# Two expert-weight loads under way instead of three, logits copied as separate work, and a new order, in a linear recurrence with a routed mixture of experts

## The chip, the cores and the metric

The kernel runs on one core of a Trainium2 chip. The metric is the device time of one execution in microseconds (us), as the median of several executions. The core has five engines with a queue of instructions each: PE (TensorE, matmuls), DVE (VectorE), ACT (ScalarE), POOL (GpSimd) and SP (SyncE, which here only issues transfers). Sixteen DMA engines move the data. An engine runs its queue strictly in order and waits at an instruction whose inputs aren't there, so that the order of each queue is the schedule.

## The reference

Two stages follow each other. The first is a gated linear recurrence over 4 sequences of 5056 tokens with 256 channels; the second sends each of the 20224 tokens to the one of eight experts with the largest logit.

```python
# recurrence, per sequence, token by token (D = 256)
log_a = 8.0 * sigmoid(r_gate) * log(sigmoid(a_param))
a = exp(log_a)
h = a * h + sqrt(max(1 - a * a, 1e-6)) * sigmoid(i_gate) * x      # x_t of the second stage
# experts, E = 8, F = 1024
logits = X @ w_gate
e = argmax(logits)
p = softmax(logits)[e];  g = sigmoid(X @ w_output_gate)[e]
out = p * g * (relu(X @ w1[e]) @ w2[e])
```

## The kernel before

The tokens are handled in 20 chunks of 8 tiles of 128 tokens, two blocks of 512 tokens in each chunk. For a chunk, SP loads `rt`, `it` and `xt` of both blocks (half a megabyte each, L536). ACT makes the gates and the decay (tanh, exp), the square of the decay (L556) and, after a table load, the root (L561); DVE makes the gate product (L548), the inputs of the recurrence (L564) and the recurrence itself as a scan (L595). PE then transposes each tile of 128 tokens and computes its logits in the same matmuls (`project`, tile `prow`, L629; three places in PSUM). From `prow` DVE takes the largest absolute value (L643) and a scale (L645), ACT or DVE writes the upper half of the row (L654 or L652), and DVE the lower half (L658) into one of eight places in `rows_all`. Just ahead of the lower half the same piece of work copies the 16 logits to `lz` (L657). From the logits of a chunk DVE and PE find experts and ranks (`pk`, L696) and DVE the positions (`posi`, L734). POOL scatters the rows by these positions into `xs` in HBM, one indirect transfer per tile (L365). From chunk 2 on each scatter waits for the newest relu, which spreads them over the time ("paced").

The second stage runs in slots of up to 256 tokens of one expert, 114 in all. Slots 0 to 7 hold 128 tokens of each expert from chunk 0, slots 8 to 15 the same of chunk 1. Later slots are dynamic: a plan made by DVE says which expert and which rows, and three plans can be in being at a time. Chunk 3 begins with slot 21, chunk 6 with 39, and chunks 7 to 11 with 43, 47, 51, 55 and 59. For a slot, SP issues a transposing fetch of the rows (L872) and one of their scales (`mt`, L873), and for dynamic slots a copy of the expert's first weights (`ws`, two of half a megabyte, L898). PE computes H in eight parts (`ph`, 48 matmuls, L929), ACT and DVE split the relu of each part into two halves (L944, L947), PE computes the output (`po`, L982), ACT scales it (L994) and POOL stores the rows (L997).

The expert weights come as 16 units, w1 and w2 of an expert by turns, 1 MB each (L424). A unit is loaded, a matmul gram gives its scale, ACT or DVE writes its upper half (L487, L489, by `MODES`: S is ACT, D is DVE), and DVE its lower half (L497). Load u waits on SP for the landing of load u - `DEPTH`, and what is behind it on SP waits too. The first 14 loads stand ahead of slot 0's fetch; the last two are staged in other places.

The order of every queue comes from a planner (`in_order`), which simulates engines and places pieces of work by rank, with durations and a table of ranks in the constants at the file's head: ranks of units, chunks, slots and loads, the slack that a projection is given, the engine of early squares and upper halves by chunk (`SQUARES`, `UPPERS`; A is ACT, D is DVE), and the chunks whose roots don't wait for both blocks (`ALONE`).

## Time and profile before

| | |
|---|---|
| median of three runs | 1082.36 us (1080.93 to 1087.27) |
| profiled execution | 1081.11 us, of which the span of the trace is 1079.4 us |
| granted PE clock, mean | 0.969 of full speed |
| PE busy | 1001.5 us, 93% |
| DVE busy | 772.4 us, 72% |
| ACT busy | 642.5 us, 60% |
| POOL busy | 361.7 us, 34% |
| moved by DMA | 250.94 MB |

The shares are means over the span. PE is far from full in the first 200 us, has a gap near 300 us, and is nearly full from there to the last 20 us. A share therefore says little here, and the rows further down go by stage. In a row of a timeline, the bracket at its end gives how long the engine had been idle, and what ended that.

### The profile page before, as it was taken

To read this page: it belongs to the slowest core of one execution; us is meant where nothing else is said; L and a number is where in the kernel's file an instruction comes from. 1 tells how busy PE (TensorE), PEld (TensorE's weight loads), DVE (VectorE), ACT (ScalarE), POOL (GpSimd) and SP (SyncE) were. 2 spreads that over 40 slices of the span, in tenths; PEclk is the share of its full clock that TensorE was granted. 3 is DMA by queue.
4 is the path that set the end of the run, shared out by engine and by line. 5 is a ranking of instruction groups with operands and counts; after the bars stand their busy time and mean duration, and the time that the engine had idled before them with its cause. 6 is when DMAs were issued, how large, how long until landed. Compare 5 with 4: busy or idle time off the path is not lost.

```text
span 1079.4 us, 31430 instructions
## 1 busy us (share of the span) xinstructions
PE 1001.5 (93%) x10506; PEld 910.0 (84%) x10506; DVE 772.4 (72%) x2324; ACT 642.5 (60%) x1153; POOL 361.7 (34%) x348
## 2 busy tenths in 40 slices
PE   3459799999989999999999999999999999999997
PEld 2358699888979889898998889889889888899996
DVE  6898989877768878888878878868776433233443
ACT  7668686867475575775776676765763323233332
POOL 1313324524324333343343343344353442121111
PEclk9659799999989999999999999999999999999999
DMA  9996447989979978879789889868855655378784
GB/s 330 382 334 131 140 121 193 239 280 291 307 211 296 258 240 261 262 228 263 238 242 265 247 239 253 252 219 259 219 178 173 190 186 157 137 223 245 240 244 125
DMA packets 200763, 250.94 MB, mean 232 GB/s; under 512 B 122108, under 2 KB 133118, under 8 KB 200608
## 3 DMA queue, kind: packets, MB, share of 16 engines
q1 hardware_dynamic: 184720, 205.55, 65.9%
q0 software_dynamic: 15888, 43.31, 12.5%
q8 instruction: 99, 1.62, 0.6%
q14 instruction: 56, 0.46, 0.1%
HBM read 79.09 MB, written 46.23 MB: 116 GB/s over the span
## 4 chain that ended last, share of the span: by engine, by line
PE 59%; issue 10%; DMA 10%; DVE 9%; POOL 5%; ACT 4%; SPq 1%; POOLq 0%; ACTq 0%; DVEq 0%
PE ph L929 27%; PE po L982 27%; PE prow L629 5%; DMA xs<-rows_all,posi 3%; POOL xs L365 3%; DVE it L595 2%; POOL out_dram L997 2%; DVE h L947 2%; DMA rt<-in_r_gate_dram 2%; DMA w2r<-in_moe_w_dram 1%; DMA ws<-w1r 1%; DMA w1r<-in_moe_w_dram 1%; DMA xt<-xs 1%; DVE it L564 1%; ACT h L944 1%
## 5 line engine op out<-in xcount | busy, mean ns | idle before, releaser
L982 PE MATMUL po<-w2r,h 128*128 (+1 forms) x3936 | 533.3, 274 | 3.5 <-ACT ot L994 1.3
L929 PE MATMUL ph<-xt,ws 128*128 128x256 f16 (+1 forms) x4704 | 484.3, 247 | 5.1 <-DMA ws<-w1r 2.1
L929 PEld LDWEIGHTS <-ws 128*128 128x128 f16 x4704 | 384.4, 98 | 42.1 <-issue 4.6
L982 PEld LDWEIGHTS <-h 128*128 128x128 f16 x3936 | 374.4, 98 | 45.4 <-issue 4.9
L947 DVE SCALAR_TENSOR_TENSOR h<-ph,h 128x256 f16<-128x256 f32 (+1 forms) x456 | 240.1, 537 | 217.6 <-ACT h L944 187.8
L944 ACT ACTIVATE h<-ph 128x256 f16<-128x256 f32 (+1 forms) x456 | 211.8, 474 | 243.1 <-PE ph L929 150.4
L997 POOL DMA_INDIRECT out_dram<-ot,mt x164 | 180.9, 1103 | 434.6 <-ACT ot L994 313.9
L365 POOL DMA_INDIRECT xs<-rows_all,posi x158 | 168.5, 1066 | 264.3 <-ACT h L944 173.2
L629 PE MATMUL prow<-iw,it 128*128 128x144 f32 x632 | 113.5, 305 | 19.7 <-DVE rows_all L658 9.9
L629 PEld LDWEIGHTS prow<-iw,it 128*128 128x128 f32 x632 | 92.4, 202 | 25.9 <-issue 10.3
L654 ACT ACTIVATE rows_all<-prow,sc 128x256 f16<-128x256 f32 x150 | 67.3, 474 | 64.0 <-DMA xs<-rows_all,posi 27.9
L994 ACT ACTIVATE ot<-po,osc 128x256 f32<-128x256 f32 x164 | 71.9, 471 | 54.9 <-PE po L982 49.4
L595 DVE TENSOR_TENSOR_SCAN it<-rt,last,it 128x512 f32<-128x512 f32 (+4 forms) x78 | 96.3, 1242 | 0.3
L658 DVE SCALAR_TENSOR_TENSOR rows_all<-prow,sc,rows_all 128x256 f16<-128x256 f32 x158 | 75.2, 477 | 0.0
L643 DVE TENSOR_REDUCE am<-prow 128x1 f32<-128x256 f32 x158 | 61.4, 418 | 17.4 <-PE prow L629 12.5
L542 ACT ACTIVATE rt<-rt 128x1024 f32<-128x1024 f32 (+1 forms) x40 | 41.8, 1045 | 34.1 <-DMA rt<-in_r_gate_dram 31.6
L552 ACT ACTIVATE rt<-rt,lam 128x512 f32<-128x512 f32 (+1 forms) x80 | 61.7, 802 | 0.5
L929 PE MATMUL ph<-xt,w1r 128*128 128x128 f16 x768 | 55.3, 225 | 4.6 <-DVE h L947 2.6
L564 DVE SCALAR_TENSOR_TENSOR it<-it,xt 128x1024 f32<-128x1024 f32 (+1 forms) x40 | 48.3, 1207 | 15.5 <-ACT it L561 15.0
L929 PEld LDWEIGHTS <-w1r 128*128 128x128 f16 x768 | 50.6, 102 | 7.3 <-issue 6.0
L548 DVE SCALAR_TENSOR_TENSOR xt<-it,xt 128x1024 f32<-128x1024 f32 (+1 forms) x40 | 48.3, 1208 | 5.8 <-ACT it L545 4.9
L545 ACT ACTIVATE it<-it 128x1024 f32<-128x1024 f32 (+1 forms) x40 | 41.9, 1048 | 8.9 <-DMA it<-in_i_gate_dram 8.5
(132 smaller groups left out, 586.0 us busy)
## 6 DMA issues: line engine op xcount, KB each, us to landing
ws<-w1r SPq DMA_DIRECT2D x196, 512.0 KB
rt<-in_r_gate_dram SPq DMA_DIRECT2D x39, 512.0 KB
it<-in_i_gate_dram SPq DMA_DIRECT2D x39, 512.0 KB
xt<-in_x_dram SPq DMA_DIRECT2D x39, 512.0 KB
w1r<-in_moe_w_dram SPq DMA_DIRECT2D x7, 1024.0 KB
w2r<-in_moe_w_dram SPq DMA_DIRECT2D x7, 1024.0 KB
out_dram<-ot,mt POOLq DMA_INDIRECT x164
xs<-rows_all,posi POOLq DMA_INDIRECT x158
```

Source lines behind the costliest of these rows:

```text
L365: op = nc.gpsimd.indirect_dma_start(out=xs[:, :], out_offset=bass.IndirectOffsetOnAxis(ap=pos, axis=0), in_=rows.bitcast(F32), in_offset=None,
L552: nc.scalar.activation(r[:, h], r[:, h], AF.Exp, scale=lam[:, h:h + 1], bias=lam[:, h:h + 1])
L595: nc.vector.tensor_tensor_scan(H[:, h, lo:hi], A[:, h, lo:hi], H[:, h, lo:hi], first, op0=ALU.mult, op1=ALU.add)
L629: nc.tensor.matmul(pf[:, h * P:(h + 1) * P + 2 * E], lhsT=H[:, h, (j % 4) * P:(j % 4 + 1) * P], rhs=iw[:, h, :], start=h == 0, stop=h == N ...
L654: nc.scalar.activation(r4(j)[:, 0], pr(j), AF.Copy, scale=sc)
L658: nc.vector.scalar_tensor_tensor(r4(j)[:, 1], pr(j), st("sc", 1, I32)[:, j, :].bitcast(F32), r4(j)[:, 0], op0=ALU.mult, op1=ALU.subtract)
L929: nc.tensor.matmul(ph[:, i, 0:w], lhsT=ws[:, f // 2 % 2, a, c, i * P:(i + 1) * P], rhs=xt[:, b * ND + c, 0:w], start=k == 0, stop=k == 3 * ...
L944: newest["relu"] = nc.scalar.activation(part(0, f0), tiles["ph", s, f0][:, :, 0:w], AF.Relu).ins
L947: nc.vector.scalar_tensor_tensor(part(1, f0), tiles["ph", s, f0][:, :, 0:w], 0.0, part(0, f0), op0=ALU.max, op1=ALU.subtract)
L982: nc.tensor.matmul(po[0:pw, j], lhsT=hh[:, a, f % 4, j * P:j * P + pw], rhs=second(b), start=f + j + a + b == 0, stop=f == NF - 1 and a == ...
L994: nc.scalar.activation(ot[0:pw], tiles["po", s][0:pw, j], AF.Copy, scale=tiles["osc", s][0:pw, j, :])
L997: op = nc.gpsimd.indirect_dma_start(out=out[:, :], out_offset=bass.IndirectOffsetOnAxis(ap=tiles["mt", s][0:pw, j, 1:2].bitcast(I32), axis=0),
```

## The change

Five things change.

- `DEPTH` is 2 instead of 3: a load of expert weights waits for the landing of the load two before it.
- Six plans can be in being (`Ring(6)`, and six buffers of `plv` and `pvi`) instead of three.
- The copy of the logits is a piece of work of its own, placed by the planner, and on ACT for chunks 0, 1, 2 and 4.
- Squares of chunks 0 and 3 and the upper halves of chunk 1 go to DVE, and units 5 and 8 change the engine of their upper halves.
- Ranks, slacks and the planner's other numbers are new, and with them the order of all queues.

ACT has 4 squares fewer, 32 copies of 128x16 more, and 8 upper halves of rows fewer; DVE has 32 copies fewer, 4 squares and 8 upper halves of rows more, two upper halves of w1 units more and one of a w2 unit less. PE and SP have as many instructions as before.

```diff
-MODES = 'SDSSSDSSSSSDSSDS'
+MODES = 'SDSSSSSSDSSDSSDS'
-SQUARES = 'AAAAA'
-UPPERS = 'AAADA'
+SQUARES = 'DAADA'
+UPPERS = 'ADADA'
+LOGITS = 'AAADA'
-LAG = 0.00125
-ALONE = (2, 5)
+LAG = 0.00118
+ALONE = (2, 6, 7)
...
-UNIT_LOAD = (7.506, 26.722, 61.465, 7.528, 72.147, 27.72, 26.183, 77.196, 87.463, 88.003, 27.858, 54.286, 26.607, 77.269, 49.185, 26.095)
+UNIT_LOAD = (-9.843, 16.647, 12.279, -35.055, -33.379, -9.228, 66.192, 67.677, -10.911, -50.334, -19.806, -7.546, -56.85, 18.29, -40.9, 67.054)
...
-DEPTH = 3
-SLACK = (1.027, 1.107)
+DEPTH = 2
+SLACK = (0.348, 1.194)
...
-        "mt": Ring(6), "ot": Ring(2), "osc": Ring(4), "plan": Ring(3), "ps_h": Ring(3), "ps_o": Ring(2), "ps_r": Ring(3),
+        "mt": Ring(6), "ot": Ring(2), "osc": Ring(4), "plan": Ring(6), "ps_h": Ring(3), "ps_o": Ring(2), "ps_r": Ring(3),
...
+        copier = "ACT" if c < len(LOGITS) and LOGITS[c] == "A" else "DVE"
...
+                def logits(j=j):
+                    lz, at = st("lz", 2 * E)[:, j, :], tiles["prow", c, j][:, P:P + 2 * E]
+                    if copier == "ACT":
+                        nc.scalar.activation(lz, at, AF.Copy)
+                    else:
+                        nc.vector.tensor_copy(lz, at)
+
                 def lo(j=j, pr=pr, r4=r4):
-                    nc.vector.tensor_copy(st("lz", 2 * E)[:, j, :], tiles["prow", c, j][:, P:P + 2 * E])
...
+                        lows.append(work(copier, 0.22 if copier == "ACT" else 0.1, logits, [w] + chain["small"], rank + TAIL, uses=[pu]))
                         w = work("DVE" if c < len(UPPERS) and UPPERS[c] == "D" else "ACT", 0.37, hi, [t, old], rank + TAIL, uses=[pu, used])
-                        lows.append(work("DVE", 0.48, lo, [w], rank + TAIL, uses=[pu, used]))
+                        lows.append(work("DVE", 0.41, lo, [w], rank + TAIL, uses=[pu, used]))
```

What the new numbers do shows in the queues. Three places follow, in each the order before and then that of the change. In the change, lines of the kernel are numbered 2 to 10 higher.

On DVE at the start, before the change, this stands between the last lower half of chunk 0's rows (`prow_7`) and chunk 0's positions (`posi_431`).

```order
L658 SCALAR_TENSOR_TENSOR rows_all<-prow_7_322,sc_285,rows_all 128x256
L678 TENSOR_REDUCE mx_385<-lz_302 128x8
L679 TENSOR_TENSOR df_387<-lz_302,mx_385 128x64
L497 SCALAR_TENSOR_TENSOR w2r<-w2r,wsc 128x2048
L686 SCALAR_TENSOR_TENSOR eq_398<-df_387,rev 128x64
...
L707 TENSOR_REDUCE zs_404<-df_387 128x8
L497 SCALAR_TENSOR_TENSOR w1r<-w1r,wsc 128x4x256
L714 TENSOR_SCALAR zs_404<-zs_404 128x8
...
L734 TENSOR_REDUCE posi_431<-pos_428 128x8
```

With the change, from the bits of the first weight scales on.

```order
L491 TENSOR_SCALAR w2r<-w2r,wsc 128x2048
L499 SCALAR_TENSOR_TENSOR w2r<-w2r,wsc 128x2048
L499 SCALAR_TENSOR_TENSOR w1r<-w1r,wsc 128x4x256
...
L499 SCALAR_TENSOR_TENSOR w1r<-w1r,wsc 128x4x256
...
L550 SCALAR_TENSOR_TENSOR xt_0_248<-it_0_180,xt_0_248 128x1024
L550 SCALAR_TENSOR_TENSOR xt_4_270<-it_4_287,xt_4_270 128x1024
...
L499 SCALAR_TENSOR_TENSOR w1r<-w1r,wsc 128x4x256 x2
...
L499 SCALAR_TENSOR_TENSOR w2r<-w2r,wsc 128x2048
...
L744 TENSOR_REDUCE posi_493<-pos_490 128x8
```

Two gate products of chunk 1, three more lower halves of w1 and one more of w2 now stand ahead of chunk 0's positions. The upper half of w2 (L489, L491) stood ahead of them before too. On SP, the 14 weight loads ahead of slot 0's fetch have ten loads of chunks 1 and 2 among them with the change, where eight stood before; on PE, seven projections of chunk 1 stand ahead of slot 0's first matmul, where four stood before.

On PE near slot 30 (`xt_30`, `ws` of the slot), before the change, the fifth projection of chunk 6 (`prow_4`) stands between the last output matmul of slot 28 and the first H of slot 30.

```order
L982 LDWEIGHTS h_1_4676
L982 ISA
L982 MATMUL po_4687<-w2r,h_1_4676 128x256
L629 MATMUL prow_4_4861<-iw,it_4_3945 128x144 x2
L929 LDWEIGHTS ws_0_4700
L929 MATMUL ph_0_4867<-xt_30_4530,ws_0_4700 128x128
```

With the change it stands inside slot 31.

```order
L939 LDWEIGHTS ws_1_4927
L939 MATMUL ph_4_5043<-xt_31_4718,ws_1_4927 128x128
L632 MATMUL prow_4_5050<-iw,it_4_3934 128x144 x2
L992 LDWEIGHTS h_0_4901
L992 ISA
L992 MATMUL po_5004<-w2r,h_0_4901 128x256
```

It has moved by more than a slot, and the projections behind it with it.

On POOL, before the change, these are the eight scatters of chunk 11 (`posi_9222`) among the stores of slots 53 to 57 (`ot_0`, `ot_1` are the halves of a slot; a slot of 128 tokens has one).

```order
L997 DMA out_dram<-ot_1_9109,mt_8365 20224x256
L365 DMA xs<-rows_all,posi_9222 172032x264 x2
L997 DMA out_dram<-ot_0_9281,mt_8560 20224x256
L365 DMA xs<-rows_all,posi_9222 172032x264 x4
L997 DMA out_dram<-ot_0_9480,mt_8918 20224x256
L997 DMA out_dram<-ot_1_9483,mt_8918 20224x256
L365 DMA xs<-rows_all,posi_9222 172032x264 x2
L997 DMA out_dram<-ot_0_9691,mt_8970 20224x256
```

With the change they are `posi_9240`.

```order
L1007 DMA out_dram<-ot_1_9118,mt_8371 20224x256
L367 DMA xs<-rows_all,posi_9240 172032x264
L1007 DMA out_dram<-ot_0_9252,mt_8532 20224x256
L367 DMA xs<-rows_all,posi_9240 172032x264 x3
L1007 DMA out_dram<-ot_0_9429,mt_8971 20224x256
L1007 DMA out_dram<-ot_1_9441,mt_8971 20224x256
L367 DMA xs<-rows_all,posi_9240 172032x264 x4
L1007 DMA out_dram<-ot_0_9624,mt_9018 20224x256
```

One scatter stood before the store of slot 54 that now stands behind it, and four instead of two stand behind the stores of slot 55.

## Rows read from the trace of the kernel before

**Rows 1.** Busy time by stage: window, length, then us (x count) per engine, clock, DMA, GB/s.
```profile
0.00:75.00 75.00, 29.81 (x216) 26.41 (x217) 61.07 (x144) 52.41 (x75) 17.52 (x26) 0.74 1.04 347
75.00:140.00 65.00, 56.01 (x654) 51.49 (x653) 58.24 (x151) 49.56 (x92) 19.96 (x13) 0.88 0.56 149
140.00:200.00 60.00, 58.51 (x756) 54.54 (x755) 53.08 (x164) 44.59 (x82) 21.00 (x19) 1.00 0.67 167
290.00:320.00 30.00, 24.95 (x271) 22.44 (x269) 18.39 (x62) 16.62 (x33) 9.04 (x9) 0.89 0.79 218
400.00:640.00 240.00, 237.84 (x2295) 214.47 (x2293) 198.24 (x617) 159.94 (x273) 87.01 (x86) 1.00 0.88 250
```
**Rows 2.** The same view, of shorter stretches (PE, PEld, DVE, ACT, POOL, clock, DMA, GB/s).
```profile
25.00:45.00 20.00, 6.44 (x67) 5.46 (x68) 17.43 (x61) 9.88 (x21) 1.57 (x1) 0.78 1.07 375
45.00:75.00 30.00, 15.59 (x98) 13.80 (x96) 29.24 (x40) 23.12 (x32) 11.31 (x7) 0.50 1.10 343
300.00:310.00 10.00, 10.00 (x93) 9.15 (x94) 8.02 (x30) 5.38 (x10) 3.35 (x4) 0.71 0.35 134
```
**Rows 3.** Chain of work that ended last, around slot 0: start us, us, what.
```profile
53.16 9.57 DMA w1r<-in_moe_w_dram
...
63.42 9.54 DMA xt<-xs
...
73.00 1.44 PE ph L929 x12
```
**Rows 4.** Timelines of ACT and DVE, chunk 0's second square, root and inputs.
```profile
13.90 1.06 ACT L556 ACTIVATE it<-rt 128x1024 f32<-128x1024 f32 x1
...
16.27 2.19 ACT L561 ACTIVATE it<-it,quarter 128x1024 f32<-128x1024 f32 x2
...
17.45 1.23 DVE L564 SCALAR_TENSOR_TENSOR it<-it,xt 128x1024 f32<-128x1024 f32 x1 [3.73 <-ACT it L561]
```
**Rows 5.** Groups of DVE, 0 to 75 us: form, count, busy us, mean ns, idle before.
```profile
L497 DVE SCALAR_TENSOR_TENSOR w1r<-w1r,wsc 128x1024 f16<-128x1024 f32 x8 | 10.1, 1277 | 0.4 <-ACT w1r L487 0.4
L497 DVE SCALAR_TENSOR_TENSOR w2r<-w2r,wsc 128x2048 f16<-128x2048 f32 x4 | 9.4, 2348 | 0.0
...
L548 DVE SCALAR_TENSOR_TENSOR xt<-it,xt 128x1024 f32<-128x1024 f32 x5 | 6.1, 1221 | 3.4 <-ACT it L545 3.0 <-DMA xt<-in_x_dram 0.4
...
L657 DVE COPY lz<-prow 128x16 f32<-128x16 f32 x10 | 1.7, 168 | 0.0
```
**Rows 6.** Timeline of DVE: chunk 0's positions, and slot 0's first lower half of H.
```profile
41.06 0.17 DVE L714 TENSOR_SCALAR zs<-zs 128x8 f32<-128x8 f32 x1 [1.85 <-ACT zs L710]
...
42.33 0.22 DVE L734 TENSOR_REDUCE posi<-pos 128x8 int32<-128x64 f32 x1
...
74.96 0.42 DVE L947 SCALAR_TENSOR_TENSOR h<-ph,h 128x256 f16<-128x256 f32 x1
```
**Rows 7.** Timeline of POOL: first and last of chunk 0's eight scatters.
```profile
43.35 1.57 POOL L365 DMA_INDIRECT xs<-rows_all,posi  x1 [32.87 <-DVE tab L743]
...
57.41 0.96 POOL L365 DMA_INDIRECT xs<-rows_all,posi  x1 [0.30 <-issue]
```
**Rows 8.** Timelines of ACT and PE at the gap near 300 us.
```profile
298.22 0.47 ACT L654 ACTIVATE rows_all<-prow,sc 128x256 f16<-128x256 f32 x1 [3.27 <-DMA xs<-rows_all,posi]
...
299.95 1.33 PE L629 MATMUL prow<-iw,it 128*128 128x144 f32 x4 [3.09 <-DVE rows_all L658]
```
**Rows 9.** Timelines of ACT, POOL, SP and PE: chunk 11 from its last relu to slot 59.
```profile
561.44 0.60 ACT L944 ACTIVATE h<-ph 128x512 f16<-128x512 f32 x1
...
563.83 0.96 POOL L365 DMA_INDIRECT xs<-rows_all,posi  x1 [0.30 <-issue]
...
569.96 1.66 SPq L872 DMA_TRANSPOSE xt<-xs  x1
...
577.08 2.13 PE L929 MATMUL ph<-xt,ws 128*128 128x256 f16 x18
```
**Rows 10.** Chain of work that ended last, a transfer of 1 KB near the end.
```profile
1056.33 3.49 DMA mt<-xs
```

More of the change, by code (lines that the diff above doesn't have):

```diff
@@ L50 @@
 SWITCH = 1.28
-LAG = 0.00125
-ALONE = (2, 5)
-QUICK = -8.31644
-ROOT = -6.82052
-EARLY = -334.613
-UNIT_RANK = (-99.063, -125.443, -110.343, -77.443, -102.247, -110.43, -95.387, -98.092, -120.534, -117.489, -77.61, -132.495, -79.534, -123.411, -78.645, -94.079)
-CHUNK_RANK = (-310.202, -0.764, -0.588, -6.533, -5.983, -12.051)
-SLOT_RANK = (-168.923, -171.768, -182.749, -176.243)
-FILL = -163.29703
-LOAD_RANK = 31.39136
+LAG = 0.00118
+ALONE = (2, 6, 7)
+QUICK = -9.2878
+ROOT = -9.65147
+EARLY = -300.04669
+UNIT_RANK = (-87.051, -170.53, -283.24, -25.864, -36.087, -254.928, -0.14, -173.046, -4.443, -21.774, -4.359, -173.007, -2.05, -214.0, -213.782, -9.006)
+CHUNK_RANK = (-329.404, -7.629, 1.571, -7.68, -8.618, -8.552)
+SLOT_RANK = (-153.944, -174.313, -196.128, -196.008)
+FILL = -233.54049
+LOAD_RANK = 4.85992
 STAGED = {14: ('ws', 'ws'), 15: ('ws', 'ws')}
 WINDOW, WARM = 3.413, (0.8, 0.35)
-UNIT_LOAD = (7.506, 26.722, 61.465, 7.528, 72.147, 27.72, 26.183, 77.196, 87.463, 88.003, 27.858, 54.286, 26.607, 77.269, 49.185, 26.095)
-CHUNK_LOAD = (-20.56, 31.524, 31.011, -14.0, -8.915, 0.024)
-TAIL = -11.96286
+UNIT_LOAD = (-9.843, 16.647, 12.279, -35.055, -33.379, -9.228, 66.192, 67.677, -10.911, -50.334, -19.806, -7.546, -56.85, 18.29, -40.9, 67.054)
+CHUNK_LOAD = (-42.752, 51.795, -36.295, -20.661, 15.923, -36.026)
+TAIL = -12.94221
 TOPS = 2
-TABLES = 49.84828
-DEPTH = 3
-SLACK = (1.027, 1.107)
+TABLES = 77.86736
+DEPTH = 2
+SLACK = (0.348, 1.194)
 SPREAD = (1.6, 2.0, 2.6)
@@ L662, in chunk @@
                 w = work("PE", 0.49, project, [states[b // 4], pold, gates], EARLY + c / 100, uses=[pu, iu], slack=SLACK[c > 3])
-                group.append((j, w, pu, old, used, hi, lo))
+                group.append((j, w, pu, old, used, hi, lo, logits))
                 if len(group) == TOPS or j == b + nb - 1:
@@ L669, in chunk @@
                     )
-                    for j, w, pu, old, used, hi, lo in group:
+                    for j, w, pu, old, used, hi, lo, logits in group:
+                        lows.append(work(copier, 0.22 if copier == "ACT" else 0.1, logits, [w] + chain["small"], rank + TAIL, uses=[pu]))
                         w = work("DVE" if c < len(UPPERS) and UPPERS[c] == "D" else "ACT", 0.37, hi, [t, old], rank + TAIL, uses=[pu, used])
-                        lows.append(work("DVE", 0.48, lo, [w], rank + TAIL, uses=[pu, used]))
+                        lows.append(work("DVE", 0.41, lo, [w], rank + TAIL, uses=[pu, used]))
                     group = []
@@ L800, in emit @@
             nc.vector.tensor_tensor_scan(bound[:, 1:E + 1], ones32[:, 0:E], own, 0.0, op0=ALU.mult, op1=ALU.add)
-            past, o = tile_of("plt", [GROUP, E + 1])[:, 0:n], tile_of("plo", [GROUP, E], bufs=3)[:, 0:n]
+            past, o = tile_of("plt", [GROUP, E + 1])[:, 0:n], tile_of("plo", [GROUP, E])[:, 0:n]
             nc.vector.tensor_tensor(past, over_e(iota_k[:, 0:n], E + 1), over_k(bound), op=ALU.is_ge)
@@ L804, in emit @@
             nc.vector.scalar_tensor_tensor(tab[:, 0, :], bound[:, 0:E], -float(w), tab[:, 3, :], op0=ALU.mult, op1=ALU.add)
-            t, v = tile_of("plf", [GROUP, 3, E])[:, 0:n, 0:m], tile_of("plv", [GROUP, 3], bufs=3)[:, 0:n, 0:m]
+            t, v = tile_of("plf", [GROUP, 3, E])[:, 0:n, 0:m], tile_of("plv", [GROUP, 3], bufs=6)[:, 0:n, 0:m]
             nc.vector.tensor_tensor(
@@ L810, in emit @@
             nc.vector.tensor_reduce(v.rearrange("p k (d a) -> p k d a", a=1), t, axis=AX.X, op=ALU.add)
-            vi = tile_of("pvi", [GROUP, 2], I32, 3)[:, 0:n]
+            vi = tile_of("pvi", [GROUP, 2], I32, 6)[:, 0:n]
             a = tile_of("pla", [GROUP, 1])[:, 0:n]
```

## The prediction

> **What bounds the kernel now.** I read the busy times by stage first, then the chain of work that ended last, then the timelines of single engines where TensorE (PE) waits. By stage [rows 1], PE is full from 400 us on (237.84 of 240). Before that it isn't: 29.81 of 75 us, 56.01 of 65, 58.51 of 60, and 24.95 of 30 us between 290 and 320. So the change can win only in the first 200 us and in that one gap; later it can only lose, by making PE wait where it doesn't now. In the first 75 us two others are full: the DMA engines, with 375 GB/s in 25 to 45 [rows 2], and from 25 us on VectorE (DVE), 17.43 of 20 and 29.24 of 30 us. The chain [rows 3] shows how the start ends: an expert load that is let go at 53.16 takes 9.57 us to 62.73, that lets the last load go, and behind it slot 0's transposing fetch is issued (63.42), lands 9.54 us later, and PE begins slot 0 at 73.00. The fetch stands behind all 14 loads in SP's queue, and behind the scatters of chunk 0, whose last is issued at 57.41 [rows 7].
>
> **The start: earlier squares, later positions.** Squares of chunk 0 leave ScalarE (ACT). The second one takes 13.90 to 14.96 just ahead of the table load and the root at 16.27, and DVE waits 3.73 us for that root [rows 4]. The trace has no 128x1024 square on DVE; the nearest row is the gate product of the same size, 1.22 us [rows 5] (bounds 1.05, as on ACT, and 1.28, the longest DVE row of that size). Two of them fit into DVE's 3.73 us of waiting, so the root comes about 1.4 us earlier (two squares of about 1.05 gone, one DVE square partly waited for). The 32 logits copies that leave DVE are short and overlap what follows: 1.7 us for ten [rows 5] is at most 0.17 each, and start to start a copy adds 0.08; for chunk 0's eight that is 0.6 to 1.4 us, and I take 0.6. On ACT a copy costs between that 0.17 and the 0.47 of an upper half, a tile sixteen times as large [rows 8]: 32 are 5 to 15 us over four chunks, beside 22.6 us in which ACT is idle in the first 75 alone [rows 1]. The eight upper halves that come to DVE (at most 0.47 each) and the splits that change engine (two upper halves of w1r more, one of w2r less, about 1.3) are 5 us of DVE behind chunk 0's positions, spread over 100 us; they count in the bounds below.
>
> Against that stands the new order. Ahead of chunk 0's positions DVE now has three more lower halves of w1r (3 x 1.28), one more of w2r (2.35) and two gate products (2 x 1.22): 8.6 us [rows 5]. Positions ended at 42.33 [rows 6]; 42.3 + 8.6 - 0.6 - 1.4 = 48.9, less the 1.85 us that DVE waited for ACT just ahead of the positions [rows 6], which the added work fills: 47. POOL's first scatter follows 1.0 behind (48.0, before 43.35), the last is issued 14.1 us later as now [rows 7], at 62.1, and with the 6.13 us from a last scatter to the fetch behind it (563.83 to 569.96, [rows 9]) slot 0's fetch comes at 68.2.
>
> SP's side comes to the same time. The 14th load now waits for the landing of the 12th, not the 11th, and two more half-megabyte chunk loads stand ahead: 2.1 MB more at 375 GB/s [rows 2] is 5.6 us, 62.73 + 5.6 = 68.3. One load fewer is then queued ahead of the fetch (1.05 MB, 2.8 us), so it lands in 9.5 - 2.8 = 6.7 us: slot 0 at 75.0, 2 us later than before. With an uncleared queue it is 77.8, with the row of an idle one (3.49, [rows 10]) 71.8. DVE, which evacuates slot 0's H first at 74.96 [rows 6], gets there between 73 and 78 by the same durations.
>
> What it buys: seven of chunk 1's eight projections now stand ahead of slot 0 (before four), so chunk 1 is routed some 15 us earlier and slots 0 to 7 share DVE with less. Between 75 and 200 us DVE sits idle 13.7 us and PE 10.5 [rows 1], mostly each waiting for the other. I set the 2 us later start against 2 us of that: **0**, bounds -8 (most of PE's idle time goes) and +6 (queue uncleared, and DVE late by 5 through slot 7).
>
> The Trainium skill ("DMA: Bandwidth & Descriptors", section "Bandwidth") speaks against fewer loads under way: a single 1 MB transfer reached 341 GB/s there, one of 16 MB 425. At 341 in place of the trace's 375 the 57 us of loads ahead of slot 0's fetch would take 5.7 more. The trace cannot say yet which it will be, since its 375 GB/s is with three loads and the chunk loads under way.
>
> **The gap at 290 to 320.** PE waits 3.09 us at 299.95 for a row of chunk 6 to be evacuated, and ACT's upper half had waited 3.27 us for a scatter of chunk 5 to free its place among the rows [rows 8]. Behind it the clock is granted at 0.71 for 10 us [rows 2], 2.9 us of full-speed work. In the new order chunk 6's fifth projection stands inside slot 31 instead of ahead of slot 30. The waiting one is the sixth: counted by the order's matmuls at full speed, 9.5 us of PE's work lay between the relu that paces the freeing scatter and it, and the wait made 12.6 of that; now 17.8 lie between. For the fourth projection it is 11.0 instead of 12.9, so some 1.6 of waiting may come up there. Most of 3.09 + 2.9 goes: **-5**, bounds 0 (chunk 5's scatters slip as much) and -8 (with the other idle time of the stretch, 5.05 us in all).
>
> **Steady chunks: shorter leads.** Tokens of a chunk must be scattered before its first slot is fetched. The scatters are paced, each behind the newest relu. For chunk 11 that relu starts at 561.44 and ends 0.60 later, the last scatter is issued at 563.83, the fetch at 569.96, slot 59 begins on PE at 577.08 without a wait [rows 9]: 15.0 us from relu to slot. In the new order the last scatter is paced by the relu four eighths of a slot later, and 24 ph and 18 po matmuls fewer lie behind it (24 x 2.13/18 from [rows 9], and 18 po of about as much): 5 us, so 10.0 are left. Needed are 0.3 (relu to scatter) + 6.13 + L, where L is from the fetch's issue to the tile. PE would wait L - 3.6 us. The trace bounds L: at most 7.1 (577.08 - 569.96, PE not waiting), at least about 3.5 (the landing in [rows 10]); 1.66 us of transposing issue [rows 9] and then that landing make 5.15, which I take, since the two follow on one another. Chunks 6, 9 and 11 have this lead: 3 x 1.55 = 4.7, **+5**. Chunks 10, 8, 7 and 3 keep 1.8 to 3.1 us more and wait for nothing at L = 5.15. At L = 7.1 it is 3 x 3.5 + 1.7 + 0.4 + 0.9 + 0.7 = 14.2; at 3.5 it is 0. From chunk 12 on the lead covers L = 7.1.
>
> The Trainium skill (same page, section "Anatomy of one DMA") puts about 2 us of fixed completion time on a transfer; with 1.66 us of issue L would be 3.7, and this term nothing. The trace's 3.49 for a transfer of 1 KB is longer than that, so I keep the row.
>
> Six plan places instead of three cost no instruction; a plan can be written earlier, which only helps. Fewer than 1 us elsewhere.
>
> **Sum** against the profiled execution: 1081.1 + 0 - 5 + 5 = 1081; the median of the three runs is 1082.4, 1.3 above that execution, so a median of 1082 is what I predict.
>
> **Rivals.**
> 1. *Leads too short* (slower). One mechanism: at chunks 6, 9 and 11 the fetch arrives 3.5 us late (L = 7.1, loads in the queue), and each wait over 3 us lowers the clock as at 300 us, 2.9 more. 1081 - 5 + 14 + 3 x 2.9 = 1099. It decides from L of about 6.3 on. For it: the DMA share is 0.88 there [rows 1]. Against it: 7.1 is only an upper bound. Chance 0.16.
> 2. *DMA under-fed at the start* (slower, mildly). With two loads under way the rate in 5 to 62 us falls from 375 to the 343 GB/s of 45 to 75 [rows 2]: 57 us become 62.6, slot 0 at 80.6, DVE idle meanwhile: 1082 + 6 = 1088. Against it: half-megabyte chunk loads are under way too. Chance 0.09. [...]
> 3. *The start runs through* (faster). Chunk 1 being ready, PE's 10.5 us of idle time in 75 to 200 goes but for 2.5; with the whole gap at 300 and L near 4: 1082 - 8 - 6 = 1068. Against it: DVE's own load is not smaller. Chance 0.26.
> 4. *Nothing reaches the end*: the gap moves rather than closes, and leads suffice: 1082. Chance 0.10.
>
> **Numbers.** Forecast 0.39, its own range 1075 to 1090. A measurement here tells about 1% from no change, 11 us. Faster than that (under 1071): most of rival 3 and a little of the forecast, 0.26. Slower (over 1093): rival 1, a third of rival 2 and a little of the forecast, 0.22. Within: 0.52. The range goes to rivals 3 and 1, 1066 to 1097: a tenth is left out at either end.
>
> **What would show it.** Right: slot 0 at 73 to 78 us with chunk 0's first scatter at about 48; chunk 1's scatters before 90; no DVE-released projection wait of 3 us at 300 and a clock near 1.0 there; PE waits of 1 to 2 us for xt ahead of the first slots of chunks 6, 9 and 11. Wrong: waits over 3 us there with a lowered clock (rival 1), less than 350 GB/s in 25 to 45 (rival 2), PE over 120 us busy between 75 and 200 (rival 3, now 114.5), or a wait in a place that I didn't name, such as the dynamic slots' weight copies or POOL's stores held up behind paced scatters.

## The result, and the profile after

The changed kernel takes 1.0066 times as long as the kernel before, with a 95% interval of 1.0048 to 1.0084 (medians 1089.1 and 1081.2 us of 20 runs each). It is slower, by some 7 us. One of the changed kernel's runs, at 1188.9 us, had a lower granted clock than the others (0.834) and isn't in the ratio. The forecast was no change (1082) with a range to 1097: the time lies inside the range and within 1%, but the sign is clear, and it was not forecast. The profiled execution took 1090.1 us, with a span of 1088.2.

Busy time by stage, changed kernel (window, length, us and count on PE, PE's weight loads, DVE, ACT and POOL, granted clock, DMA share, GB/s). They answer to [rows 1], but for 200 to 290 and 640 to 800 us, which those rows didn't cover.

```profile
0.00:75.00 75.00, 31.88 (x213) 28.62 (x214) 63.62 (x144) 55.06 (x87) 14.14 (x26) 0.72 1.01 353
75.00:140.00 65.00, 49.67 (x595) 45.69 (x595) 57.60 (x127) 38.95 (x80) 17.96 (x12) 0.85 0.56 139
140.00:200.00 60.00, 59.05 (x785) 55.87 (x784) 54.87 (x166) 42.93 (x85) 20.47 (x18) 1.00 0.60 158
200.00:290.00 90.00, 81.31 (x1003) 74.30 (x1001) 70.16 (x237) 56.59 (x121) 33.70 (x31) 1.00 0.96 277
290.00:320.00 30.00, 27.99 (x340) 25.85 (x338) 23.82 (x75) 18.48 (x34) 11.67 (x10) 1.00 0.95 291
...
400.00:640.00 240.00, 237.22 (x2291) 214.28 (x2289) 193.53 (x598) 163.00 (x274) 88.44 (x85) 1.00 0.88 247
640.00:800.00 160.00, 153.81 (x1396) 137.26 (x1395) 125.20 (x359) 106.41 (x174) 59.63 (x57) 0.99 0.77 232
```

The same view of the kernel before, for those two stages.

```profile
200.00:290.00 90.00, 85.77 (x1037) 78.00 (x1036) 73.39 (x251) 60.56 (x117) 35.49 (x31) 0.98 1.03 295
...
640.00:800.00 160.00, 157.24 (x1439) 140.77 (x1437) 125.28 (x359) 108.49 (x178) 64.00 (x59) 1.00 0.78 233
```

PE lost 6.3 us of busy time between 75 and 140 us and 4.5 between 200 and 290, won 3.0 in the gap near 300, and lost 3.4 between 640 and 800. In the second and the last of these stages the prediction expected nothing. The loss of the second shows as six waits of 0.9 to 1.6 us. It isn't this execution's alone: the twelve profiles of the changed order have 81.3 to 85.6 us there (mean 83.2), five of the kernel before's order 85.0 to 86.2.

The start, by the chain of work that ended last of the changed kernel (answers to [rows 3]).

```profile
59.87 8.31 DMA w2r<-in_moe_w_dram
...
68.88 8.13 DMA xt<-xs
...
77.05 0.80 PE ph L939 x6
```

Slot 0's fetch and first matmul come 5.5 and 4.1 us later than before. Timelines of DVE and POOL, changed kernel: chunk 0's inputs, positions and first scatter (answer to [rows 4, 6, 7]).

```profile
15.54 1.23 DVE L566 SCALAR_TENSOR_TENSOR it<-it,xt 128x1024 f32<-128x1024 f32 x1 [0.61 <-ACT it L563]
...
49.05 0.22 DVE L744 TENSOR_REDUCE posi<-pos 128x8 int32<-128x64 f32 x1
```
```profile
50.08 0.96 POOL L367 DMA_INDIRECT xs<-rows_all,posi  x1 [39.61 <-DVE wsc L465]
```

The inputs come 1.9 us earlier (15.54, before 17.45), the positions 6.7 us later.

Then there is a hole that the prediction didn't know. Timelines of DVE and PE, changed kernel, near 95 us:

```profile
92.27 2.36 DVE L550 SCALAR_TENSOR_TENSOR xt<-it,xt 128x1024 f32<-128x1024 f32 x2
98.04 0.16 DVE L465 TENSOR_SCALAR wsc<-pg 128x1 int32<-128x1 int32 x1 [3.41 <-remote]
...
98.25 5.06 PE L992 MATMUL po<-w2r,h 128*128 128x256 f16 x23 [4.92 <-issue]
```

DVE waits 3.41 us ahead of the scale of a weight, and the view calls what ended the wait "remote". PE's output matmul, whose place in PSUM that scale frees, waits behind it. What DVE waits for can be told: its instruction waits for one semaphore, which PE raises at the end of the gram's sum. The profile models the ends of those matmuls, at 93.11 and 93.34; the trace also records when the semaphore was raised, and that was at 98.02 and 98.06. So it was PE that got there late, by 4.7 us. While it idles its granted clock falls to one half. Busy time just behind the hole, changed kernel and then a_same (the same kernel on another chip, without a hole):

```profile
98.00:104.00 6.00, 5.75 (x31) 4.16 (x31) 4.76 (x9) 2.82 (x4) 0.13 (x1) 0.50 0.07 25
```
```profile
98.00:104.00 6.00, 5.35 (x68) 4.71 (x66) 5.86 (x13) 4.95 (x9) 5.39 (x3) 1.00 0.25 67
```

A second wait belongs to the new order. Timeline of PE, changed kernel:

```profile
131.47 1.46 PE L939 MATMUL ph<-xt,w1r 128*128 128x128 f16 x12 [5.57 <-DVE h L957]
```

DVE does two upper and three lower halves of w1 ahead of that half of H. All twelve profiles of the changed order have this wait at 5.57 us, with two loads or three; the kernel before waits 3.1 to 4.0 us nearby for a row.

Near 300 us the gap is closed: the projection that waited 3.09 us [rows 8] now waits 0.42. But two projections further on wait as that one did. Timelines of ACT and PE, changed kernel:

```profile
299.03 0.76 PE L632 MATMUL prow<-iw,it 128*128 128x144 f32 x4 [0.42 <-DVE rows_all L667]
...
685.43 0.47 ACT L657 ACTIVATE rows_all<-prow,sc 128x256 f16<-128x256 f32 x1 [3.75 <-DMA xs<-rows_all,posi]
...
686.57 0.73 PE L632 MATMUL prow<-iw,it 128*128 128x144 f32 x4 [2.26 <-DVE rows_all L667]
...
725.96 0.47 ACT L657 ACTIVATE rows_all<-prow,sc 128x256 f16<-128x256 f32 x1 [5.34 <-DMA xs<-rows_all,posi]
...
727.01 0.76 PE L632 MATMUL prow<-iw,it 128*128 128x144 f32 x4 [2.76 <-DVE rows_all L667]
```

It is the chain of [rows 8] word for word: ACT waits for a scatter to free a row's place, DVE for ACT, PE for DVE.

At chunk 11 the tokens arrive in time. Timelines of ACT, POOL, SP and PE, changed kernel (answer to [rows 9]):

```profile
569.98 0.60 ACT L954 ACTIVATE h<-ph 128x512 f16<-128x512 f32 x1 [0.60 <-issue]
...
570.85 0.96 POOL L367 DMA_INDIRECT xs<-rows_all,posi  x1 [0.96 <-ACT h L954]
...
573.47 1.35 SPq L882 DMA_TRANSPOSE xt<-xs  x1
...
580.54 1.47 PE L939 MATMUL ph<-xt,ws 128*128 128x256 f16 x12
```

From the relu's end to slot 59 it is 9.96 us (15.0 before), and PE still doesn't wait.

### The profile page after: what moved, and what is told of

Same layout as the page of the kernel before. It is cut to its first block, busy times and chain, and to the rows that moved or that the text cites. A ratio compares the mean times of both kernels' runs of the same rounds, so it can differ in the third digit from the quotient of the medians.

```text
span 1088.2 us, 31531 instructions
## 1 busy us (share of the span) xinstructions
PE 997.5 (92%) x10506; PEld 907.5 (83%) x10506; DVE 779.6 (72%) x2305; ACT 637.8 (59%) x1172; POOL 356.7 (33%) x348
## 4 chain that ended last, share of the span: by engine, by line
PE 42%; issue 16%; DMA 15%; DVE 11%; ACT 9%; POOL 5%; SPq 2%; POOLq 0%; another core or an unknown queue 0%; ACTq 0%; DVEq 0%
PE ph L939 20%; PE po L992 19%; DMA w1r<-in_moe_w_dram 4%; DMA rt<-in_r_gate_dram 4%; DMA xs<-rows_all,posi 3%; PE prow L632 3%; POOL xs L367 3%; DVE it L597 2%; POOL out_dram L1007 2%; DVE h L957 2%; ACT h L954 2%; DMA out_dram<-ot,mt 1%; ACT it L563 1%; DVE it L566 1%; ACT L563 1%
## 5 line engine op out<-in xcount | busy, mean ns | idle before, releaser
L992 PE MATMUL po<-w2r,h 128*128 (+1 forms) x3936 | 549.1, 274 | 8.0 <-issue 6.4
L939 PE MATMUL ph<-xt,ws 128*128 128x256 f16 (+1 forms) x4704 | 498.1, 247 | 11.4 <-DVE h L957 3.5
L939 PEld LDWEIGHTS <-ws 128*128 128x128 f16 x4704 | 387.4, 98 | 50.5 <-DMA ws<-w1r 7.6
L992 PEld LDWEIGHTS <-h 128*128 128x128 f16 x3936 | 371.4, 98 | 47.9 <-issue 9.2
L1007 POOL DMA_INDIRECT out_dram<-ot,mt x164 | 176.9, 1079 | 448.7 <-ACT ot L1004 280.3
L367 POOL DMA_INDIRECT xs<-rows_all,posi x158 | 167.5, 1060 | 258.9 <-ACT h L954 155.9
L632 PE MATMUL prow<-iw,it 128*128 128x144 f32 x632 | 111.1, 305 | 18.3 <-DVE rows_all L667 13.9
L667 DVE SCALAR_TENSOR_TENSOR rows_all<-prow,sc,rows_all 128x256 f16<-128x256 f32 x158 | 72.2, 478 | 31.0 <-ACT rows_all L657 29.6
L657 ACT ACTIVATE rows_all<-prow,sc 128x256 f16<-128x256 f32 x142 | 63.2, 474 | 46.4 <-DMA xs<-rows_all,posi 33.2
```

The source lines that it names most:

```text
L367: op = nc.gpsimd.indirect_dma_start(out=xs[:, :], out_offset=bass.IndirectOffsetOnAxis(ap=pos, axis=0), in_=rows.bitcast(F32), in_offset=None,
L632: nc.tensor.matmul(pf[:, h * P:(h + 1) * P + 2 * E], lhsT=H[:, h, (j % 4) * P:(j % 4 + 1) * P], rhs=iw[:, h, :], start=h == 0, stop=h == N ...
L657: nc.scalar.activation(r4(j)[:, 0], pr(j), AF.Copy, scale=sc)
L667: nc.vector.scalar_tensor_tensor(r4(j)[:, 1], pr(j), st("sc", 1, I32)[:, j, :].bitcast(F32), r4(j)[:, 0], op0=ALU.mult, op1=ALU.subtract)
L939: nc.tensor.matmul(ph[:, i, 0:w], lhsT=ws[:, f // 2 % 2, a, c, i * P:(i + 1) * P], rhs=xt[:, b * ND + c, 0:w], start=k == 0, stop=k == 3 * ...
L992: nc.tensor.matmul(po[0:pw, j], lhsT=hh[:, a, f % 4, j * P:j * P + pw], rhs=second(b), start=f + j + a + b == 0, stop=f == NF - 1 and a == ...
```

## The experiments

The chips differ: the kernel before has medians from 1068.7 to 1079.9 us on them. So each kernel is compared by its ratio to the kernel before on its own chip, and kernels with each other only where they ran on one.

| chip | kernel | median us | ratio to before (95% interval) |
|---|---|---|---|
| A (before 1079.9) | a_depth3 | 1076.6 | 0.9972 (0.9952 to 0.9992) |
| A | b_depth2 | 1081.3 | 1.0012 (0.9983 to 1.0041) |
| A | a_rows9 | 1079.2 | 0.9989 (0.9960 to 1.0018) |
| A | b_rows9 | 1070.9 | 0.9919 (0.9895 to 0.9943) |
| B (before 1076.4) | a_first3 | 1080.0 | 1.0040 (1.0006 to 1.0074) |
| B | a_last3 | 1083.5 | 1.0065 (1.0027 to 1.0103) |
| B | a_depth3_again | 1075.7 | 1.0013 (0.9975 to 1.0051) |
| B | a_depth3_rows9 | 1069.1 | 0.9938 (0.9904 to 0.9972) |
| C (before 1068.7) | b_again | 1067.7 | 1.0002 (0.9963 to 1.0041) |
| C | a_again | 1071.0 | 1.0023 (0.9994 to 1.0051) |
| C | a_sq_lz | 1071.5 | 1.0017 (0.9989 to 1.0045) |
| C | b_new_rows9 | 1069.7 | 1.0009 (0.9987 to 1.0031) |
| D (before 1078.2) | a_same | 1082.4 | 1.0068 (1.0038 to 1.0099) |
| D | a_depth3_same | 1078.3 | 1.0010 (0.9981 to 1.0039) |
| D | a_rows9_same | 1077.0 | 0.9995 (0.9963 to 1.0027) |
| D | b_rows9_same | 1068.0 | 0.9917 (0.9889 to 0.9944) |

Names that begin with a are made from the changed kernel, with b from the kernel before. All but b_new_rows9 keep the order that the planner made for the kernel that they are made from (in a_sq_lz the moved pieces stand in another engine's queue). The changed kernel itself ran on C and D, but not on A and B.

Where a step of one order is compared over several executions, these are the times between two stores of results on POOL, from the timelines, in us. Within one order, the same work lies between the two.

| kernel | store of slot 3 | slots 27 to 33 | slots 64 to 66 |
|---|---|---|---|
| before | 117.8 | 57.9 | 24.3 |
| b_again, b_depth2 | 117.3, 120.4 | 50.4, 51.6 | 23.5, 25.9 |
| b_rows9, b_rows9_same | 117.9, 117.7 | 50.5, 50.7 | 25.0, 24.5 |
| changed | 126.0 | 49.2 | 31.8 |
| a_again, a_same, a_sq_lz | 120.2, 119.4, 120.9 | 50.3, 48.2, 48.7 | 31.9, 32.0, 31.3 |
| a_first3, a_last3 | 119.5, 125.7 | 49.9, 49.5 | 30.4, 31.7 |
| a_depth3, _again, _same | 119.5 in each | 49.9, 49.4, 49.0 | 31.5, 31.6, 31.0 |
| a_rows9, a_rows9_same | 126.5, 119.6 | 49.3, 49.7 | 27.0, 26.7 |
| a_depth3_rows9 | 119.5 | 47.9 | 26.7 |

**The number of loads under way.** a_depth3 (run again as a_depth3_again and a_depth3_same) gives the changed kernel its third load back.

```diff
-                if u >= DEPTH:
+                if u >= 3:
...
-                        ins.ins, tiles["load", u - DEPTH].name,
+                        ins.ins, tiles["load", u - 3].name,
```

> The changed kernel with every queue in the same order; only the wait of a weight load is for the landing three before it again, not two. Theory (order): the 5 us that the changed kernel is behind at slot 3 come from DVE's order at the start, not from the number of loads under way. Slot 0's fetch stays bound by chunk 0's scatters and begins between 66 and 69 us, its landing is 1 to 3 us longer with one load more in the queue, slot 0 begins at 76 to 79 us (changed kernel 77.0), and the time is within 3 us of the changed kernel, 1086 to 1092. Rival (loads): two loads under way starve the start; with three, slot 0 begins at 72 to 74 us and the time falls by 4 to 6 us, to 1083 to 1085.

> The changed kernel with three loads under way once more, for a profile nearer to its median: the profiled execution so far was 1089.4 us where the median of 13 is 1076.6. Slot 0's store of results is as early as there (5 us ahead of the changed kernel by slot 3), and the later stages do not lose the 10 us that the slow execution lost between slots 35 and 77; by slot 77 it stays 6 us or more ahead of the changed kernel. If it loses them again, the lead of the start is given back later, and the 12 us between the medians have another source.

b_depth2 is the reverse edit on the kernel before (2 for 3).

> The kernel before with every queue in the same order; only the wait of a weight load is for the landing two before it, not three. Theory (order): the last load is issued one landing later (2 to 3 us), its fetch lands that much faster, slot 0 begins at 72 to 75 us (before 73.0), and the time is within 3 us of the kernel before, 1078 to 1084. Rival (loads): the DMA engines move less than 350 GB/s between 25 and 45 us, slot 0 begins at 77 us or later and the time is 4 to 6 us longer, 1085 to 1087.

The kernel before shows no clear loss: 1.0012, slot 0 at 74.8 us, 374 GB/s in 25 to 45 us. The changed kernel does: with three loads it equals the kernel before or better (0.9972, 1.0013, 1.0010), with two it is at 1.0066. So the theory that the order alone costs the time fell. But slot 0 doesn't move: it begins at 75.6 and 75.7 us with three loads (expected 72 to 74 by the rival), and at 75.4 in a_same with two. What differs at slot 3 is the hole near 95 us. The profile of a_depth3 was of an execution 13 us above its median, and so told little of the later stages. That of a_depth3_again (1078.8 us) stays 6 to 13 us ahead of the changed kernel's from the store of slot 3 to the end, as expected. Against the kernel before's profile it is 10.4 us ahead at the store of slot 64 and 1.7 at the last; part of that goes to the same two waits for row places (1.97 and 3.17 us).

Busy time between 45 and 60 us, changed kernel and then a_depth3_same.

```profile
45.00:60.00 15.00, 8.51 (x67) 7.64 (x67) 13.07 (x34) 14.85 (x21) 8.10 (x7) 0.50 0.99 330
```
```profile
45.00:60.00 15.00, 8.52 (x67) 7.65 (x67) 13.19 (x33) 14.88 (x21) 8.28 (x7) 0.50 1.06 387
```

The rate is 330 GB/s with two loads and 387 with three (over all profiles of this order 330 to 371 and 387 to 389). In this stretch only one chunk load stands between the weight loads, and chunk 0's scatters run from 50 us on. Between 25 and 45 us, with chunk loads among them, both reach 381. A low rate alone doesn't cost the time: b_depth2 has 358 GB/s in the same stretch, the kernel before 389.

a_first3 and a_last3 split that edit: three under way only for loads 0 to 11, or only for the last four.

```diff
-                if u >= DEPTH:
+                near = 3 if u < 12 else 2
+                if u >= near:
```

> The changed kernel in the same order; loads 0 to 11 of the expert weights wait for the landing three before them, the last four still for the landing two before. It tells apart what two loads under way cost in the changed order (12 us by the medians so far: 1089 with two, 1077 with three). Theory (SP blocked at the end): the cost comes from the last two loads ahead of slot 0's fetch, which SP issues at 65.0 and 68.2 us with two under way and at 61.2 and 63.4 with three, and the fetch stands behind them. Then this kernel gains at most 3 us: 1086 to 1089, last load at 66 us or later, and PE and DVE still idle for 3 to 5 us near 95 us. Rival (rate over the whole start): loads land late from 40 us on because two under way don't fill the DMA engines (330 GB/s in 45 to 60 us against 389), and the splits with them; then this kernel gains nearly all, 1076 to 1080.

> The changed kernel in the same order; only the last four loads of the expert weights (two ahead of slot 0's fetch, and the two staged ones behind it) wait for the landing three before them, the others for two. Theory (SP blocked at the end): nearly all of the 12 us comes back, 1076 to 1080, with the last load issued before 66 us and no idle DVE near 95 us. Rival (rate over the whole start): at most 3 us come back, 1086 to 1089.

a_last3 gains nothing (1.0065), though its last load is issued at 63.4 us instead of 68.2; it has the hole, and its store of slot 3 is as late as the changed kernel's. a_first3 has no hole and is at 1.0040. By the medians, then, the first twelve loads are part of what costs, and SP's blocked end is not. But the intervals of a_first3, a_last3 and a_depth3_again, all on chip B, overlap, so that neither is shown.

**The changed kernel again.** a_again and a_same are unchanged.

> The changed kernel once more, unchanged, for a second profile and more times beside the kernel before on the same chip. Theory: DVE and PE sit idle for 3.5 to 5 us from about 94 us on, as in all three kernels of this order whose first twelve loads went two at a time and in none of the four with three; slot 3 is 5 to 7 us behind the kernel before, and the projections near 686 and 727 us wait 2 to 3 us. The ratio to the kernel before is 1.005 to 1.008.

> The changed kernel, unchanged, on one chip with the next three. By 20 runs its ratio to the kernel before is 1.0066, on another chip by 8 runs 1.0023. Theory (two causes): the step of 6 to 7 us between the stores of slots 64 and 66, which all five kernels of this order with eight places showed on three chips, is there whatever the chip; the idle 3.5 to 5 us near 95 us may be there or not. Ratio 1.002 to 1.004 if they are not, 1.006 to 1.008 if they are.

On chip C the changed kernel is at 1.0023 and has no hole, on chip D it is at 1.0068 and its profiled execution, the fastest of twelve, has none either. So both expectations missed: without a hole in the profile the ratio was to be 1.002 to 1.004. Of seven profiles with the first twelve loads two at a time three show the hole (changed, a_last3, a_rows9), of five with three at a time none. Twelve profiles are few: a split like this comes about by chance one time in six. It could also go by the chip, since none of the five profiles on C and D has a hole. In a_depth3_same the same DVE instruction follows at once (timeline of DVE):

```profile
91.22 2.38 DVE L550 SCALAR_TENSOR_TENSOR xt<-it,xt 128x1024 f32<-128x1024 f32 x2
93.52 0.15 DVE L465 TENSOR_SCALAR wsc<-pg 128x1 int32<-128x1 int32 x1
```

> The changed kernel in the same order with three loads under way. Theory (two causes): if a_same shows the idle time near 95 us, this one does not, and is 4 to 6 us faster than a_same; if a_same does not show it, the two are within 2 us. Rival (the third load is worth it by itself, through the rate of the start): it is 4 us or more faster than a_same in either case.

On chip D the third load is worth 4.1 us by the medians (1082.4 and 1078.3); the two intervals just touch. By the letter of the expectation its rival came out, since the profile of a_same has no hole. Yet the two profiles don't show the rate at work either. They are level at the stores of slot 3 (119.4 and 119.5) and slot 20 (232.8 and 233.3), and that of a_same is the fastest of its twelve executions. What the other executions of a_same lose wasn't seen. So it is shown that the third load is worth some 4 us in this order on that chip, and not how: whether it is the hole in some executions stays open, and so does what makes PE late there.

**A ninth place for rows.** a_rows9 and b_rows9 (again as a_rows9_same and b_rows9_same) give the scattered rows nine places, at the old order. A piece of SBUF that is only written had to be halved for it.

```diff
-ROWS = 8
+ROWS = 9
...
-"rows": Ring(ROWS)
+"rows": Ring(8)
...
-            dg = small.tile([P, P], F32, name=f"dg_{u}", tag="dg", bufs=1)
+            dg = small.tile([P, P], BF16, name=f"dg_{u}", tag="dg", bufs=1)
```

> The changed kernel with nine places for scattered rows instead of eight, and every queue in the same order (the squares of a gram, which nothing reads, are written in half the width to make room). Theory (row places): the projections that wait 2.3 us at 686.6 and 2.8 us at 727.0 in the changed kernel wait because the upper half of a row waits for a scatter to free its place. With one place more, that scatter is one earlier (about 2 to 4 us): these two waits fall below 1 us each, what the changed kernel loses between slots 64 and 71 (5 us) goes, and the time is 4 to 6 us shorter, 1083 to 1085. Rival: the scatter's place isn't what they wait for (the number of places in PSUM, or ACT's own queue): the waits stay and the time is within 2 us of the changed kernel.

> The changed kernel in the same order with two loads under way and nine places for scattered rows. Theory: the step between the stores of slots 64 and 66 is 3 us or less instead of 6 to 7, and it is 5 to 9 us faster than a_same (ratio to the kernel before 0.996 to 0.999).

Both waits are gone, in all three profiles with nine places; a_rows9 has four others of at most 1.4 us (3.9 in all). PE's waits by releaser between 130 and 1060 us, in all, times, longest: changed, a_same, a_rows9_same.

```profile
PE prow L632 <- DVE rows_all L667: 8.4, 8, 2.8
```
```profile
PE prow L632 <- DVE rows_all L667: 6.1, 8, 1.6
```
```profile
PE prow L632 <- DVE rows_all L667: 0.4, 1, 0.4
```

From the store of slot 64 to that of 66 all nine profiles of the changed order with eight places have 30.4 to 32.0 us, on every chip, and the three with nine 26.7 to 27.0. That is 5 us for a row's place at chunk 15, and it is shown: one place more, and the 5 us are gone. On chip D the time falls by 5.5 us in all (1082.4 to 1077.0). That the whole 5.5 is this one step is not shown, since the same edit gains more in the kernel before, which has no such step.

> The kernel before with nine places for scattered rows instead of eight, and every queue in the same order (the squares of a gram written in half the width to make room). Theory (row places): PE's wait of 3.1 us at 300 us and the granted clock of 0.71 behind it go without any change of order, 4 to 6 us of the 1081, so 1075 to 1077. Rival: the gap at 300 us needs the new order; the wait stays above 2 us and the time within 2 us of the kernel before.

> The kernel before in its own order with nine places for scattered rows. On one chip it was 9 us faster than the kernel before (0.992). If that is the gap near 300 us and small waits after it, as its profile there suggested, the gain depends on how often the gap opens: 0.990 to 0.994 on a chip on which the kernel before takes 1076 us or more, and 0.997 to 1.000 on one on which it takes 1069.

The kernel before gains more by the same place, 0.9919 and 0.9917, and its step from slot 64 to 66 doesn't change. Row places thus cost both kernels about the same, and don't account for the difference between them. The waits of the kernel before, in the same window: before, and b_again on chip C.

```profile
PE prow L629 <- DVE rows_all L658: 5.1, 3, 3.1
```
```profile
PE prow L629 <- DVE rows_all L658: 1.6, 3, 0.9
```

> The kernel before once more, unchanged, for a second profile. The prediction took 5 us for the gap near 300 us from one profiled execution, which lost 10.7 us between the stores of slots 27 and 33 against full-speed work; the same order with two loads under way lost 4.4 there. If the gap is typical, this execution shows a projection that waits 3 us for a row's place near 300 us with the granted clock below 0.8 behind it, and 9 to 11 us lost between those slots. If it was an accident of that execution, 3 to 6 us.

The second profile of the kernel before has no gap near 300 us. Its projection there, in PE's timeline, waits 0.89 us:

```profile
290.38 0.76 PE L629 MATMUL prow<-iw,it 128*128 128x144 f32 x4 [0.89 <-DVE rows_all L658]
```

Slots 27 to 33 take 50.4 us, as in b_depth2 (51.6) and with nine places (50.5, 50.7). The 57.9 us of the execution that the prediction read were the exception among three. Why b_rows9 gains a whole 10 us on chip D is not settled by these waits. On chip A the gain lies late: from the store of slot 33 to the last, b_depth2 (eight places) takes 738.9 us and b_rows9 730.9, where b_depth2's waits for places are 5.5 us in six. On chip C b_again takes 731.5 with eight; b_rows9 was not run there.

a_depth3_rows9 puts both edits together.

> The changed kernel in the same order with three loads under way and nine places for scattered rows. If the two losses are separate (start: 12 us; projections that wait for a row's place near 686 and 727 us: 5 to 10 us), the gains add: 1089 - 12 - 8 = 1069, range 1066 to 1072, which is below the kernel before with nine places (1070.9) if the new order is worth something by itself. If they are not separate (a late start and late chunks are the same loss), 1075 to 1078.

0.9938, and 1069.1 us, which is the theory of two separate losses to the microsecond. That the number fits so well is luck, since it was added up from medians of different chips. By the ratios of chip D the two gains add as well: 1.0068, less 0.0058 for the third load and 0.0073 for the place, is 0.9937. The kernel before with nine places is at 0.9919 and 0.9917, so no run shows a gain of the new order by itself.

**The moved pieces of work.** a_sq_lz has the early squares on ACT and all logits copies on DVE again.

```diff
-            def square(t=t, by=SQUARES[c] if c < len(SQUARES) else "A"):
+            def square(t=t, by="A"):
...
-                    if copier == "ACT":
-                        nc.scalar.activation(lz, at, AF.Copy)
-                    else:
-                        nc.vector.tensor_copy(lz, at)
+                    nc.vector.tensor_copy(lz, at)
```

> The changed kernel in the same order, but the squares of chunks 0 and 3 on ACT again and all logits copies on DVE again. It measures what these moves are worth by themselves. Theory (as predicted: the root comes 1.4 us earlier and the copies cost 0.6 us of DVE ahead of chunk 0's positions): chunk 0's first scatter comes 1 to 3 us later than in the changed kernel (51 to 53 us instead of 50.1), and the time is 0 to 3 us longer. Rival: DVE has the weights' lower halves to do in between, which fill the gap; the first scatter comes at 50 to 50.5 us and the time is the same within 2 us.

POOL's first scatter of chunk 0, in a_sq_lz and then in a_again on the same chip:

```profile
51.91 0.96 POOL L367 DMA_INDIRECT xs<-rows_all,posi  x1 [42.46 <-DVE wsc L465]
```
```profile
50.00 0.96 POOL L367 DMA_INDIRECT xs<-rows_all,posi  x1 [40.53 <-DVE wsc L465]
```

It is 1.9 us later, against 2.0 predicted (1.4 for the root and 0.6 for the copies), but not by those parts: chunk 0's inputs alone come 2.9 us later (19.00 and 16.08). The time is the same within its interval (1071.5 and 1071.0).

**The general numbers alone.** b_new_rows9 has the kernel before's ranks for the start, three loads and nine places, and the change's numbers for the steady part; here the planner makes a new order.

```diff
-LAG = 0.00125
-ALONE = (2, 5)
-QUICK = -8.31644
-ROOT = -6.82052
+LAG = 0.00118
+ALONE = (2, 6, 7)
+QUICK = -9.2878
+ROOT = -9.65147
...
-LOAD_RANK = 31.39136
+LOAD_RANK = 4.85992
...
-TAIL = -11.96286
+TAIL = -12.94221
...
-SLACK = (1.027, 1.107)
+SLACK = (1.027, 1.194)
```

> The kernel before with three loads under way and its own order of the start, with the change's general numbers (the slack of projections from chunk 4 on, the lag, the ranks of roots, loads and rows, and the chunks whose roots wait for one block), and nine places for scattered rows. By the order, 8.8 to 14.7 us of PE's work lie between a scatter and the projection that reuses its place in chunks 9 to 12 (before: 9.5 to 12.8), and 18 to 22 us between the last scatter and the next chunk's first slot (before: 16). Theory: the steady waits for rows and for fetched tokens shrink further, and it is 1 to 4 us faster than the kernel before with nine places: ratio 0.988 to 0.991. Rival: with nine places nothing waits any more in the steady part, and the ratio is that of the kernel before with nine places, 0.992.

1.0009 on chip C, neither of the two numbers expected. The start didn't stay that of the kernel before: PE waits 4.70 us for an expert load at 131.8 us, and the store of slot 7 is at 163.7 us (151.2 in b_again on the same chip). From the store of slot 20 to the last the two take 826.8 and 826.3 us, so that the ninth place and the longer leads together gave nothing there. Since the kernel before with nine places didn't run on chip C, the run doesn't tell the two apart.

## Why the prediction failed

**The start** was set at 0, bounds -8 and +6. Its parts held. The root came 1.9 us earlier (1.4 predicted), positions at 49.05 (47), the first scatter at 50.08 (48.0), the last load was issued at 68.20 (68.3), slot 0's fetch at 68.88 (68.2), and PE began at 77.05 (75.0, bound 77.8). Chunk 1 was scattered from 92.05 us on rather than 101.80. The trade, "2 us later start against 2 us of that", held too, as long as there was no hole: the store of slot 3 is then at 119.4 to 120.9 us (before 117.3 to 117.9), but that of slot 20 at 230.9 to 234.6 (before 230.6 to 238.0). The step that failed is that the third load was priced as a later slot 0 and nothing else. The swap of that load alone is worth 4.1 us on chip D, and with it the changed kernel is level with the kernel before. In the profile with the result the start shows a hole instead: PE late by 4.7 us near 95 us, its clock at one half behind it, the store of slot 3 at 126.0 and that of slot 20 at 239.7. Whether the hole is what the third load takes away stays open.

Rival 2, chance 0.09, had the direction. It looked for a low rate in 25 to 45 us, where the rate is 381; the rate is lower with two loads in 45 to 60 us, and no run shows that this is what was paid. The Trainium skill (page "DMA: Bandwidth & Descriptors", section "Bandwidth") gives 341 GB/s for a single transfer of 1 MB. Two loads under way beside chunk loads moved 381 here, and 330 to 371 where only one chunk load stood among them.

**The gap near 300** was set at -5. The mechanism was right in the trace (0.42 us of waiting, clock 1.00). The size was not the change's to give: it was read from one execution, and two others of the same order did not have it. For the median of executions the term is a fraction of 5; how large a fraction was not measured.

**The steady leads** were set at +5. The lead was computed to 10.0 us and measured 9.96. The need was mis-sized: 6.13 us from the last scatter to the fetch was taken for what a fetch needs, but now it follows 2.62 us after the scatter's issue, and PE doesn't wait. All waits for fetched tokens after 130 us together are 0.5 us. The term is 0.

**What was missed** are the row places: 5 us at chunk 15, between the stores of slots 64 and 66, and a wait of some 3 us at chunk 16 in five of the nine profiles with eight places. This is a term that the prediction put at nothing ("Fewer than 1 us elsewhere"). It had named the chain at 300 us, and counted PE's work between the pacing relu and the reusing projection for that place alone; it said that from chunk 12 on the leads suffice, and meant the fetch leads. Of its signs of being wrong, "a wait in a place that I didn't name" is the one that came.

**The sum**, by the stores of the two profiled executions (changed less before): 5.4 us lost up to slot 27, 8.7 won from slot 27 to 33, 3.4 lost from there to slot 64, 7.6 lost from slot 64 to 66, and 1.7 lost to the last store, 9.3 in all. At slot 64 the two are level, as forecast, and that is luck: a start with a hole stood against an exceptional gap. It is luck too that the forecast is within 1%: the 5 us for the leads, which didn't come, stood in for the 5 us of row places, which did.

**A version that beats both** came out of the study: the kernel before with nine places for rows, 0.9917 and 0.9919.

## What to carry to other kernels

When a stall's mechanism is found at one place, count the same slack at every place of the new order where the same resource is reused; a new order closes one gap and opens the next, and one more buffer can be worth more than either order (here a ninth row place). A stall read from a single profiled execution says little of the median; a second profile of the unchanged kernel, which costs little, didn't have it. When a view can't name what ended a wait, ask which engine raises the semaphore: a matmul's end in the profile is modelled, and PE can be the late one. A time between two events is a latency only if nothing else held the second one back: look at what stood ahead of it in its queue.

## What was not expected of the hardware

Four chips gave medians of 1068.7 to 1079.9 us for the same kernel, 1.0%. And an instruction fetch of 8 KB stood in the DMA queues longer with two loads under way: 2.2% to 3.7% of the DMA engines' time in 88 to 91 us in four profiles looked at here (changed, a_last3, a_same, a_again), 0.7% in a_depth3_same. It doesn't go with the hole, though. DMA by queue in that window, the changed kernel with a hole and a_again without one:

```profile
q14 instruction: 1, 0.01, 3.2%
```
```profile
q14 instruction: 1, 0.01, 3.7%
```
